# Attention masks and one table of query scales: loaded, or made on the chip from one row

## The chip, the cores and the metric

The kernel runs on one core of one Trainium2 chip. The metric is the device time of one execution in microseconds (us). Inputs lie in the chip's memory in the layouts that the host gave them; the host does no arithmetic on data.

## The reference, cut to what matters

```python
def _attn_ref(q, k, v):                     # (2, 8, 768, 64) each
    gamma = 1.0 - 2.0 ** (-5.0 - np.arange(H))
    for t in range(S):
        state = gamma * state + k[t] outer v[t]         # 64 x 64 per batch and head
        y[:, :, t] = scale * q[:, :, t] @ state
...
x = y as (1536 tokens, 512)
x = softplus(x @ moe_w_in) @ moe_w_out      # 512 -> 2048 -> 512
return silu(x @ moe2_w_in) @ moe2_w_out     # 512 -> 2048 -> 512
```

The first stage is retention: attention whose weight between token t and an earlier token s is gamma^(t-s), with one gamma for each of the eight heads. Two feed-forward layers follow.

## The kernel before

Retention is done in chunks of 128 tokens: two batches of six chunks are twelve tiles n = 0 to 11, n % 2 the batch, n // 2 the chunk. For each tile att_scores(n) (L263) multiplies keys by queries for the eight heads into two PSUM banks, four heads (one j of each head pair) in each; att_mask(n) (L271, VectorE) multiplies the two banks by mask[:, j], which holds scale * gamma^(t-s) for t >= s and 0 elsewhere; att_within(n) (L281) multiplies the result by the values; att_split(n) copies the sum out in two parts (L325 on ScalarE, L330 on VectorE). From chunk 1 on att_across (L303) adds what earlier chunks contribute: the queries, scaled by the table qs[c] (L215, on GpSimd for the early tiles), times the running state, which att_state (L243) sums from scaled keys (L230, factors in `cs`). att_turn_k (L223) turns the keys of the first tiles by a product with an identity, and ScalarE copies them out (L224). The scaled keys of tiles 0 and 1 come from GpSimd, later ones from VectorE.

The feed-forward layers follow (L529 and L569 the first; L679 and L713 the second), on weights that VectorE and ScalarE take apart from 64-bit floats (L427 to L474); the first weight tile is done between the masks and the key scales of tiles 2 and 3.

The order is written by hand (manual_schedule): each engine works through its instructions in the order of the code, and each waits for what it needs. All loads are issued from SP's queue, in the order of the code, at most eight ahead: the ninth waits until the first has landed, and so on. The first are

```python
att_load(0, 0, 2)                                # queries and keys of tile 0
nc.sync.dma_start(out=mask, in_=mask_d)          # 512 KB
att_load(1, 0, 2)
nc.sync.dma_start(out=cs, in_=cs_d)              # 24 KB
```

and behind them values and keys of tiles 0 and 1, queries and keys of 2 and 3, qs_load(1) (256 KB), and the first weight tile. While they are on their way TensorE runs WARM = 3 products of zeros (L889), 128 x 512 in float32, and GpSimd makes the identity (L877). Then, on TensorE: att_scores(0), att_turn_k(0), att_scores(1), att_within(0), att_within(1), att_scores(2), att_scores(3), att_state(0), att_state(1), att_within(2), att_within(3), att_across(2), att_state(2), att_state(3), and the first product of the first feed-forward layer.

att_scores(n) writes into the PSUM banks acc0 and acc1 for even n, acc2 and acc3 for odd n.

## Time and profile before

| | us |
|---|---|
| median of three runs | 562.45 (562.42 to 562.97) |
| the profiled execution | 562.56 |
| its span | 560.8 |
| TensorE busy in the span | 555.0 (99%) |
| VectorE busy | 346.8 (62%) |
| ScalarE busy | 295.1 (53%) |
| GpSimd busy | 39.1 (7%) |

Times in the rows below are microseconds from the start of the span. 1.8 us of the profiled execution lie outside its span. PE is TensorE and PEld its loading of weights, DVE is VectorE, ACT ScalarE, POOL GpSimd, SP the queue that issues the loads. A matrix product in float32 stands as two instructions. The ends of products are modelled, so that one that is followed at once by another is shown with an end that lies in the other; the distance between two starts is the safer number.

### The profile page before, as it was taken

How to read it: one execution, taken by the hardware profiler on the slowest of the kernel's cores; microseconds unless marked ns; L12 is line 12 of the kernel's file. 1: busy time of each engine (PE TensorE's matmuls, PEld its weight loads, DVE VectorE, ACT ScalarE, POOL GpSimd, SP SyncE). 2: the span in 40 equal slices, each digit the busy share in tenths (PEclk: the TensorE clock that was granted, in tenths of full speed). 3: DMA queues.
4: the chain of work that ended last, by engine and by line, in shares of the span. 5: the costliest groups of instructions: out<-in, count | busy, mean ns of one | idle time of the engine just before them, and what ended most of it. 6: DMA issues, size and time to landing. Idle time of an engine off the chain costs nothing.

```text
span 560.8 us, 8160 instructions
## 1 busy us (share of the span) xinstructions
PE 555.0 (99%) x3130; PEld 478.1 (85%) x3130; DVE 346.8 (62%) x618; ACT 295.1 (53%) x534; POOL 39.1 (7%) x56
## 2 busy tenths in 40 slices
PE   8999999999999999999999999999999999999997
PEld 6888888888888888888888989989889999999995
DVE  3999866699998989897953878525332221222113
ACT  2455535776776867876844867434524332332322
POOL 2321000010000101010200011000000000000000
PEclk9999999999999999999999999999999999999999
DMA  8993242497797678866835798764521554444412
GB/s 302 398 413 130 82 181 77 176 350 280 272 346 273 228 261 348 279 247 223 285 137 200 266 415 339 274 230 180 207 75 57 188 199 162 161 143 176 193 75 112
DMA packets 29062, 125.31 MB, mean 223 GB/s; under 512 B 3296, under 2 KB 3296, under 8 KB 25312
## 3 DMA queue, kind: packets, MB, share of 16 engines
q1 hardware_dynamic: 22752, 101.74, 49.0%
q0 software_dynamic: 6272, 23.07, 10.9%
q8 instruction: 24, 0.39, 0.3%
q14 instruction: 14, 0.11, 0.1%
HBM read 98.58 MB, written 26.21 MB: 223 GB/s over the span
## 4 chain that ended last, share of the span: by engine, by line
PE 97%; DMA 2%; SPq 0%; DVE 0%; issue 0%
PE acc L713 24%; PE h L529 24%; PE acc L569 23%; PE by L679 9%; PE bx L679 6%; PE bz L679 6%; DMA rp<-in_att 2%; PE py L281 2%; PE sc L263 1%; PE py L303 1%; PE state L243 1%; DVE rp L720 0%; SPq L858 0%; SPq L208 0%; SPq L393 0%
## 5 line engine op out<-in xcount | busy, mean ns | idle before, releaser
L529 PE MATMUL h<-rx,rw 128*128 128x512 f32 (+1 forms) x588 | 137.6, 386 | 0.0
L569 PE MATMUL acc<-rg,rw 128*128 128x512 f32 x564 | 134.6, 389 | 0.0
L529 PEld LDWEIGHTS h<-rx,rw 128*128 128x128 f32 x588 | 108.5, 188 | 22.4
L713 PE MATMUL acc<-rw,rg 128*128 128x512 f32 x477 | 125.3, 392 | 0.0
L569 PEld LDWEIGHTS acc<-rg,rw 128*128 128x128 f32 x564 | 105.7, 188 | 21.6 <-issue 0.2
L713 PEld LDWEIGHTS acc<-rw,rg 128*128 128x128 f32 x477 | 88.5, 188 | 12.6
L698 DVE TENSOR_TENSOR rg<-re,rg 128x384 fp32r<-128x384 f32 x53 | 29.4, 556 | 90.9 <-ACT re L696 90.9
L548 ACT ACTIVATE rg<-h 128x512 fp32r<-128x512 f32 x47 | 27.9, 595 | 65.0 <-PE h L529 51.1
L427 ACT ACTIVATE rc<-rc 128x512 f32<-128x512 f32 x58 | 38.5, 670 | 13.5 <-DMA rc<-in_wts 8.0
L445 DVE SCALAR_TENSOR_TENSOR rc<-rc 128x512 uint32<-128x512 uint32 x58 | 40.2, 693 | 2.0
L695 ACT ACTIVATE rg<-by 128x384 fp32r<-128x384 f32 x16 | 7.9, 491 | 54.2 <-PE by L679 54.2
L442 DVE TENSOR_SCALAR rc<-rc 128x512 uint32<-128x512 uint32 x64 | 27.4, 428 | 13.0 <-ACT rc L427 12.9
L768 DVE TENSOR_TENSOR rp<-bz,rp 128x384 f32<-128x384 f32 x16 | 8.9, 557 | 39.3 <-PE bz L679 39.3
L555 DVE TENSOR_TENSOR rg<-re,rg 128x512 fp32r<-128x512 f32 x47 | 32.1, 686 | 1.7 <-ACT re L549 1.6
L679 PE MATMUL by<-f,rw 128*128 128x384 f32 x144 | 29.2, 337 | 0.0
L679 PE MATMUL by<-rx,rw 128*128 128x384 f32 x144 | 29.2, 337 | 0.0
L448 DVE TENSOR_SCALAR rc<-rc 128x512 uint32<-128x512 uint32 x64 | 27.3, 427 | 2.2
L431 ACT ACTIVATE rc<-rc 128x1024 uint16<-128x1024 uint16 x27 | 28.5, 1055 | 0.0
L549 ACT ACTIVATE re<-h 128x512 f32<-128x512 f32 x48 | 28.4, 593 | 0.0
L679 PEld LDWEIGHTS by<-f,rw 128*128 128x128 f32 x144 | 25.9, 188 | 2.0
L679 PEld LDWEIGHTS by<-rx,rw 128*128 128x128 f32 x144 | 25.8, 188 | 2.2 <-ACT by L753 0.2
L474 ACT ACTIVATE rw<-rc 128x512 fp32r<-128x512 f32 x32 | 20.2, 632 | 13.2 <-DVE rc L445 13.2
(104 smaller groups left out, 699.1 us busy)
## 6 DMA issues: line engine op xcount, KB each, us to landing
rc<-in_wts SPq DMA_DIRECT2D x58, 512.0 KB, 4.5
rw<-d SPq DMA_DIRECT2D x13, 1792.0 KB, 7.3
rw<-d SPq DMA_DIRECT2D x14, 1024.0 KB, 9.1
near<-in_wts SPq DMA_DIRECT2D x21, 511.5 KB, 3.8
d<-st POOLq DMA_DIRECT2D x16, 512.0 KB, 6.0
d<-st POOLq DMA_DIRECT2D x8, 1024.0 KB, 5.1
rp<-in_att SPq DMA_DIRECT2D x8, 512.0 KB, 7.2
d<-w POOLq DMA_DIRECT2D x8, 512.0 KB, 3.8
```

The source lines that it names most:

```text
L427: nc.scalar.activation(out=z, in_=raw(u)[:, :, 1].bitcast(F32), func=AF.Copy, scale=2.0**-112)
L431: nc.scalar.activation(out=q[:, :, 0:2], in_=q[:, :, 1:3], func=AF.Copy)
L442: nc.vector.tensor_scalar(out=z, in0=z, scalar1=3, scalar2=4, op0=ALU.logical_shift_left, op1=ALU.bitwise_or)
L445: nc.vector.scalar_tensor_tensor(out=a, in0=hi, scalar=0x80000000, in1=z, op0=ALU.bitwise_and, op1=ALU.bitwise_or)
L529: nc.tensor.matmul(ph[:, t], lhsT=w[:, s], rhs=x[:, kc, t], start=kc == o == j == 0, stop=kc == NPAIR - 1 and j == 2, skip_group_check=i == 0,
L548: nc.scalar.activation(out=ghi, in_=ph, func=AF.Softplus)
L549: nc.scalar.activation(out=t, in_=ph, func=AF.Softplus)
L555: nc.vector.tensor_tensor(out=glo, in0=t, in1=ghi.bitcast(F32), op=ALU.subtract)
L569: nc.tensor.matmul(acc_t[m], lhsT=lhsT, rhs=rhs, start=first and j == 0 and not seeded, stop=last and j == 2, skip_group_check=m in SEEDED,)
L679: nc.tensor.matmul(to, lhsT=a[:, s], rhs=x[:, kc, :], start=start and kc == j == 0, stop=kc == 1 and j == 2, skip_group_check=True,)
L698: rest[c] = lambda: nc.vector.tensor_tensor(out=glo, in0=r, in1=ghi.bitcast(F32), op=ALU.subtract)
L713: nc.tensor.matmul(acc2_t[m], lhsT=a[:, s], rhs=b, start=start and j == 0, stop=stop and j == 2)
```

## The change

Neither the mask nor the query scales of chunk 1 are loaded. One partition's row of the mask (row 0: scale * gamma^t for every head, 4 KB) is loaded instead, from ScalarE's queue, and `cs` behind it from the same queue. A new function tables_make multiplies a row of ones by that row on TensorE, once for each j, which puts the row into all 128 partitions of a PSUM bank. VectorE makes from it and from `cs` the factor gamma^-s of each partition and head (`decay`) and multiplies; GpSimd puts zeros where t < s. ScalarE copies the row, one token further, as the query scales of chunk 1 into the two 64-partition halves, and VectorE makes their last column. The two banks are those of acc2 and acc3, which att_scores(1) takes next. WARM is 1, and att_turn_k(0) stands behind att_mask(1).

```diff
-WARM = 3
+WARM = 1
...
+    ones = rr[0:1, 1152 : 1152 + P]
+    decay = rr[:, 1280 : 1280 + H].rearrange("p (j a) -> p j a", j=2)
+    mask_row = rr[0:1, 8192:9216].rearrange("p (j t) -> p j t", j=2)
...
+    def rows_load():
+
+        nc.scalar.dma_start(out=mask_row, in_=mask_d[0:1].rearrange("p j a t -> p j (a t)"))
+        nc.scalar.dma_start(out=cs, in_=cs_d)
+
+    def tables_make():
+
+
+        grow = cs[:, H : 2 * H].rearrange("p (a j) -> p j a", j=2)
+        row = [psa.tile([P, NPAIR, P], F32, tag=f"acc{2 + j}", name=f"row{j}") for j in range(2)]
+        qs_t[1] = qs_ring.next()
+        qs = _rows(qs_t[1], NPAIR)
+        root = float(D) ** 0.5
+        for j in range(2):
+            nc.tensor.matmul(row[j], lhsT=ones, rhs=mask_row[:, j], start=True, stop=True)
+        for j in range(2):
+            r = slice(j * D, (j + 1) * D)
+            nc.vector.scalar_tensor_tensor(
+                out=decay[:, j], in0=row[j][:, :, 1], scalar=root, in1=grow[:, j], op0=ALU.mult, op1=ALU.mult
+            )
+            nc.vector.tensor_tensor(
+                out=mask[:, j],
+                in0=row[j],
+                in1=decay[:, j].rearrange("p (a o) -> p a o", o=1).to_broadcast([P, NPAIR, P]),
+                op=ALU.mult,
+            )
+            nc.scalar.activation(out=qs[r, :, : P - 1], in_=row[j][r, :, 1:], func=AF.Copy)
+            nc.vector.scalar_tensor_tensor(
+                out=qs[r, :, P - 1], in0=qs[r, :, P - 2], scalar=root, in1=row[j][r, :, 1], op0=ALU.mult, op1=ALU.mult
+            )
+            nc.gpsimd.affine_select(
+                out=mask[:, j],
...
     with tc.manual_schedule():
         att_load(0, 0, 2)
-        nc.sync.dma_start(out=mask, in_=mask_d)
         att_load(1, 0, 2)
-        nc.sync.dma_start(out=cs, in_=cs_d)
+        rows_load()
...
-        qs_load(1)
...
+        nc.vector.memset(ones, 1.0)
...
+        tables_make()
         att_scores(0)
         att_mask(0)
-        att_turn_k(0)
         att_scores(1)
         att_mask(1)
+        att_turn_k(0)
```

In the changed file lines stand further down: L263 is L306 there, L223 L266, L271 L314, L281 L324, L230 L273.

On TensorE the program begins before the change as follows (sc0 and sc1 are the scores of tiles 0 and 1, their second number is j; kn0 the turned keys of tile 0, py0 and py1 the outputs of att_within).

```order
L889 MATMUL warm_119<-rr_76 128x512 x3
L263 MATMUL sc0_0_123<-rp_67 128x128
...
L263 MATMUL sc0_1_124<-rp_67 128x128
L223 MATMUL kn0_135<-rr_76,rp_67 128x128 x4
L263 MATMUL sc1_0_141<-rp_67 128x128
...
L263 MATMUL sc1_1_142<-rp_67 128x128
L281 MATMUL py0_153<-rr_76,rp_67 64x128 x8
L281 MATMUL py1_166<-rr_76,rp_67 64x128 x8
```

And after it:

```order
L931 MATMUL warm_119<-rr_76 128x512
L221 MATMUL row0_121<-rr_76 128x512
L221 MATMUL row1_122<-rr_76 128x512
L306 MATMUL sc0_0_135<-rp_67 128x128
...
L306 MATMUL sc0_1_136<-rp_67 128x128
L306 MATMUL sc1_0_147<-rp_67 128x128
...
L306 MATMUL sc1_1_148<-rp_67 128x128
L266 MATMUL kn0_159<-rr_76,rp_67 128x128 x4
L324 MATMUL py0_165<-rr_76,rp_67 64x128 x8
L324 MATMUL py1_178<-rr_76,rp_67 64x128 x8
```

Two warm-up products have given way to the two row products, and the turned keys stand behind the scores of tile 1.

On VectorE, between the clearing of rr_76 and the first copy of an output, with what each waits for (DMAHW: a transfer; row0 and row1 are the two banks), stands after the change:

```order
L224 SCALAR_TENSOR_TENSOR rr_76<-row0_121,cs_72 128x4 [waits DMAHW2_49,PE_49]
L227 TENSOR_TENSOR rr_76<-row0_121,rr_76 128x512 [waits DVE_49]
L234 SCALAR_TENSOR_TENSOR rr_76<-rr_76,row0_121 64x4 [waits Activation_49]
L224 SCALAR_TENSOR_TENSOR rr_76<-row1_122,cs_72 128x4 [waits PE_49]
L227 TENSOR_TENSOR rr_76<-row1_122,rr_76 128x512 [waits DVE_49]
L234 SCALAR_TENSOR_TENSOR rr_76<-rr_76,row1_122 64x4 [waits Activation_49]
L314 TENSOR_TENSOR rr_76<-sc0_0_135,rr_76 128x512 [waits PE_49,Pool_49]
L314 TENSOR_TENSOR rr_76<-sc0_1_136,rr_76 128x512 [waits PE_49,Pool_49]
```

Before, the two mask products of tile 0 were the first work behind the clearing; now six instructions stand ahead of them, and they wait for GpSimd too, where before the first of them waited for the mask's transfer.

ScalarE begins after the change with (the table load was first before):

```order
L209 DMA rr_76<-in_mask 1x1024
L210 DMA cs_72<-in_cs 128x48
L915 ACT_TABLE_LOAD
L233 ACTIVATE rr_76<-row0_121 64x4x127 [waits DVE_49]
L233 ACTIVATE rr_76<-row1_122 64x4x127 [waits DVE_49]
L267 ACTIVATE rp_67<-kn0_159 128x512 [waits PE_49]
```

Two issues stand ahead of the table load, and two copies of the rows, each behind VectorE's mask product of the same bank, ahead of the copy of the turned keys.

## Rows read from the trace of the kernel before

**Rows 1.** Busy time by stretch; columns: stretch, length, engines, granted clock, DMA share, GB/s.
```profile
1.46:6.52 5.06, 5.06 (x7) 1.85 (x7) 0.00 (x0) 0.57 (x1) 0.00 (x0) 1.00 0.88 277
6.52:15.73 9.21, 8.73 (x138) 7.73 (x137) 6.01 (x10) 2.58 (x5) 4.08 (x4) 1.00 1.03 380
15.73:21.00 5.27, 5.23 (x97) 4.74 (x97) 5.09 (x10) 3.54 (x6) 0.50 (x1) 1.00 1.03 401
21.00:540.00 519.00, 519.00 (x2813) 449.34 (x2814) 329.85 (x590) 282.81 (x514) 33.79 (x46) 1.00 0.61 225
```

**Rows 2.** The chain of waits of 0 to 22 us: start, length, what.
```profile
1.65 6.20 DMA rp<-in_att
...
8.24 7.36 DMA rp<-in_att
```

**Rows 3.** TensorE's timeline: start, length, instructions [idle time before them, releaser].
```profile
1.46 5.13 PE L889 MATMUL warm<-rr 128*128 128x512 f32 x6 [1.46 <-DVE rr L875]
6.52 1.16 PE L263 MATMUL sc<-rp 64*128 64x128 f32 x16
7.61 1.16 PE L223 MATMUL kn<-rr,rp 128*128 128x128 f32 x8
8.70 1.16 PE L263 MATMUL sc<-rp 64*128 64x128 f32 x16
9.79 2.53 PE L281 MATMUL py<-rr,rp 128*64 128x128 f32 x32
12.25 1.16 PE L263 MATMUL sc<-rp 64*128 64x128 f32 x16
...
15.73 1.09 PE L281 MATMUL py<-rr,rp 128*64 128x128 f32 x16 [0.34 <-DMA rp<-in_att]
...
17.62 1.96 PE L303 MATMUL py<-rr 64*64 64x128 f32 x32
19.52 0.93 PE L243 MATMUL state<-rp,rr 128*64 128x64 f32 x15
```

**Rows 4.** Waits of 0 to 21 us: who for whom, sum in us, times, longest.
```profile
PEld sc L263 <- issue: 1.3, 2, 1.1
...
PE py L281 <- DMA rp<-in_att: 0.3, 1, 0.3
...
PEld state L243 <- DVE rr L230: 0.2, 1, 0.2
```

**Rows 5.** VectorE's timeline of the same stretch.
```profile
12.99 0.69 DVE L330 TENSOR_TENSOR rx<-py,rx 128x512 fp32r<-128x512 f32 x1 [0.73 <-ACT rx L325]
13.60 2.48 DVE L271 TENSOR_TENSOR rr<-sc,rr 128x512 f32<-128x512 f32 x4
...
18.68 0.69 DVE L230 TENSOR_TENSOR rr<-rp,cs 128x512 f32<-128x512 f32 x1
```

**Rows 6.** SP's timeline: start of an issue, its length.
```profile
0.74 0.38 SPq L208 DMA_DIRECT2D rp<-in_att  x1
...
2.12 0.52 SPq L860 DMA_DIRECT2D cs<-in_cs  x1
```

**Rows 7.** DMA issues of the first 1 and 2.5 us: count, KB each, us to landing.
```profile
rp<-in_att SPq DMA_DIRECT2D x1, 512.0 KB, 4.5
...
cs<-in_cs SPq DMA_DIRECT2D x1, 24.0 KB, 5.9
```

**Rows 8.** What the DMA engines moved, 0 to 10 us in 40 slices of 0.25 us.
```profile
GB/s 0 0 0 0 0 0 0 180 115 295 246 213 246 180 262 328 311 279 295 344 328 410 377 377 410 349 402 373 288 231 241 156 221 336 410 401 426 418 410 467
```

**Rows 9.** Groups of instructions of 0 to 16 us: count, busy us, mean ns, idle before.
```profile
L271 DVE TENSOR_TENSOR rr<-sc,rr 128x512 f32<-128x512 f32 x8 | 5.1, 684 | 7.2 <-PE sc L263 7.2
...
L224 ACT ACTIVATE rp<-kn 128x512 f32<-128x512 f32 x1 | 0.6, 597 | 6.8 <-PE kn L223 6.8
...
L877 POOL TENSOR_SCALAR_AFFINE_SELECT rr<-rr 128x128 f32<-128x128 f32 x1 | 0.3, 292 | 0.1
```

More of the change, by code (lines that the diff above doesn't have):

```diff
@@ L202, in qs_load @@
         nc.sync.dma_start(out=qs_t[c], in_=qs_d[c])
+    def rows_load():
[26 more added lines that the diff above has]
+                out=mask[:, j],
+                in_=mask[:, j],
+                compare_op=ALU.is_ge,
+                fill=0.0,
+                base=0,
+                pattern=[[0, NPAIR], [1, P]],
+                channel_multiplier=-1,
+            )
     def att_load(n, lo=0, hi=4):
```

## The prediction, made before the changed kernel ran

> **What bounds the kernel now.** I read four views in this order. First the busy time by stretch [rows 1]: from 21 us to 540 us TensorE is busy 519.00 of 519.00 us, so nothing that happens on another engine or queue there can be seen in the time, and whatever moves the first 21 us moves the end by the same amount. Between 6.52 and 21 us TensorE is idle 0.52 us in all (9.21 less 8.73, 5.27 less 5.23). Before 6.52 us it runs only the three warm-up products on zeros. Second the chain of waits of the first 22 us [rows 2]: it is laid through two loads from `in_att`, 6.20 and 7.36 us long, up to 15.6 us. That reads as if the loads bound the start. Third the TensorE timeline and the waits [rows 3, 4], which show that this is only half of it: the load held TensorE 0.3 us at 15.73 us, and next to it TensorE was as good as full. Fourth VectorE [rows 5]: it stands 0.73 us until ScalarE has copied the output of token tile 1, starts the subtraction at 12.99 us, and from 13.60 us works on without a pause to L230 at 18.68 us, for which TensorE waits at 19.52 us (0.2 us, [rows 4]). So two chains end at 19.5 us: the loads, which let go at 15.73 us, and "att_within(1) ends, ScalarE, VectorE", which starts where TensorE goes over to att_scores(2), at 12.25 us [rows 3]. To gain, a change must bring both forward; to lose, it is enough to delay one.
>
> **The bytes taken off the SP queue.** The mask (512 KB) and the query scales of chunk 1 (256 KB) are gone, 0.79 MB. At the 380 GB/s of 6.52 to 15.73 us [rows 1] that is 2.1 us, so the loads behind them land about 1.3 us (behind the mask) to 2.1 us earlier. What this is worth: the 0.3 us stall at 15.73 us, if TensorE comes there as early as now. What is late next is VectorE, at 19.52 us, so of the 2.1 us nearly nothing is left. SP's other loads move up with it and wait for less. GpSimd's first query scaling no longer waits for a load; its result is wanted only by att_across(2) at 17.6 us, so this is worth 0.
>
> **The warm-up.** Three products of 128 x 512 in float32 stand as six instructions in 5.13 us, 0.855 us each, 1.71 us a product [rows 3]. L223 right behind them runs eight instructions of 128 columns between 7.61 and 8.70 us, 0.545 us for 512 columns. So the warm-up runs at the lower of TensorE's two levels (1.2 GHz) and the work behind it above that, although the granted clock reads 1.00 in both stretches [rows 1]. WARM = 1 takes out two products, 3.42 us. tables_make puts in two products of the same 512 columns (one row deep instead of 128). Taken at the warm-up's price, as the nearest row with the same columns at that place, they cost 3.42 us again: the sum is zero, if the first can start when the single warm-up ends, at 1.46 + 1.71 = 3.17 us.
>
> **When it can start.** It waits for the mask's first row, 4 KB on ScalarE's queue, which is issued as SP's first load is, at about 0.74 us [rows 6]. Bytes first move in the slice that starts at 1.75 us [rows 8], 1.0 us after the first issue. From the last byte to the landing: by the sums of [rows 8] (slices of 0.25 us) 524 KB had moved at about 4.0 us, and the first load (524 KB, issued at 0.74 us, 4.5 us on its way [rows 6, 7]) landed at 5.24 us, so 1.2 us. The least is therefore 0.74 + 1.0 + 1.2 = 2.94 us, hidden by the warm-up; the most, if it goes at the pace of the full load beside it, is 5.24 us, 2.1 us after the warm-up. I take 0.4 us of sharing, 3.35 us, nearer to the low end because only 4 KB have to move. The second transfer, `cs`, took 5.9 us behind 1.57 MB in SP's queue [rows 7]; now it is issued at about 1.15 us and lands between 3.35 us (1.0 + 1.2 later) and 7.05 us (5.9 later). It is wanted when the first row product is done, 3.35 + 1.71 + 0.07 = 5.13 us. I take it as just in time; each microsecond later costs one.
>
> **The chain that makes the tables.** Per half: a VectorE product of 4 columns, a mask product of 512 columns (0.68, the mean of L271 [rows 9]), a ScalarE copy (0.60, as L224 [rows 9]), a VectorE fix of 4 columns. The waits order them strictly: the ScalarE copy waits for the mask product, the fix for the copy. No row has a VectorE instruction of 4 columns: between 0 and the 0.68 of 512 columns, I take 0.16, near the low end for its size. With 0.18 for the hand-overs (0.03 to 0.05 each, from the gap between 7.68 us, when att_scores(0) ends, and the next engine's starts) a half is 1.78 us. The first half, from 5.13 us, ends at 6.91 us, as the second row product does (3.35 + 3.42 + 0.07 = 6.84 us): almost hidden. The second half is open: 6.84 + 1.78 = 8.62 us. Who waits for it: att_scores(1) writes into the two banks of the row products, so its second matmul stands until the second fix. TensorE has done att_scores(0) by 7.9 us and idles 0.7 us there. Behind it, in TensorE's queue, stands everything else.
>
> **The masks' triangles.** Two GpSimd selections of 512 columns. The only row is 128 columns in 0.292 us [rows 9]; times four 1.17 us. The second starts at about 7.8 us and is done at 9.0 us; VectorE asks for it at 9.3 us (fixes done at 8.62 us, then the first product of att_mask(0), 0.68), and att_within(1) does not need the last mask product before 11.7 us where VectorE can give it at 11.3 us. Cover 0.3 + 0.4 us: the selection would have to take about 2 us to cost anything.
>
> **The sum.** 8.62 us; the other 15 of 16 matmuls of att_scores(1) 1.02 (of 1.09, [rows 3]) gives 9.64; att_turn_k(0), which now stands behind it, 1.09 gives 10.73; att_within(0) and (1) 1.89 (what att_within(2) and (3) take without a wait between them, 15.73 to 17.62 us [rows 3]) and the 0.2 us pause of issue before att_scores(2) (1.3 less 1.1, [rows 4]) give 12.82 us, against 12.25 us. That is 0.57 us later. VectorE's row from 12.99 to 19.5 us starts at that point and has no gap to give it back, and behind 21 us TensorE has none either. Profiled execution: 562.56 + 0.57 = **563.1 us**. The median of the three runs is 562.45, 0.11 below it; I leave that in the range.
>
> **A page of the skill beside it.** The transfers on ScalarE's queue decide the sum, and no row shows a small one beside a full SP queue. The Trainium skill, DMA: Bandwidth & Descriptors (Queues, rings and completion order), says that each DMA engine takes turns between the queues it has work for, a packet at a time. By that rule both small transfers would pass SP's bytes and land near the low ends, the row product would start at 3.17 us, and the sum would be 562.9 us (0.18 less).
>
> **The rivals.**
> - *The small transfers come late.* Place: TensorE in front of the row products, or VectorE's first product for `cs`. For it: loads issued in the first 3 us took 4.5 to 5.9 us [rows 7], and the DMA engines move no more than 277 GB/s in that stretch [rows 1]. Against it: they are small. Price: one to one from 3.17 us for the row and from about 5.1 us for `cs`. It decides, slower by more than 0.2% (1.12 us, about what a measurement of this kernel can tell from no change), from a landing at about 3.9 us or 5.7 us. A row at 4.5 us gives 564.3; the ends (5.24, 7.05) give 565.0 and 565.0.
> - *TensorE's clock stays low longer.* Now the engine works without a break from 1.46 to 6.5 us before it runs faster. After the change it pauses up to 0.2 us at 3.2 us and 0.7 us at 7.9 us, and the row products fill one row of the array. If the faster level comes only behind that, att_scores(1), att_turn_k(0) and att_within(0) and (1) (1.02 + 1.09 + 1.89 = 4.0 us) run up to 1.57 times as long (0.855 against 0.545, [rows 3]): up to +2.3 us, 565.4; att_scores(1) alone, +0.6, 563.7. The Trainium skill, TensorE: Matmul & The Clock Gate (What's actually happening), says that the slow level is the default and activity releases it; by that the two pauses count against the change.
> - *The loads were the bound after all.* The chain of waits speaks for it [rows 2], and then up to 2.1 us come off: 560.5. Against it: in front of 15.73 us TensorE has only 0.5 us of idle time to close [rows 1], and the new chain adds a pause. At best the row products start at 3.17 us, run faster at their end and the stall goes: 562.0, which is within 0.2%.
> - *GpSimd's selection takes over 2 us*, from which it decides; at 2.5 us each the second ends at 11.4 us where 9.7 us (9.0 and the cover) would do: 1.7 us late, 564.8.
>
> **How the numbers follow.** The forecast with its neighbours within 0.2%: 0.60. Late transfers 0.21, of which 0.17 slower by more; low clock 0.11, of which 0.09; slow selection 0.05, all of it; loads as the bound 0.03, faster by more. That is 0.60 + 0.04 + 0.02 = 0.66 within 0.2%, 0.17 + 0.09 + 0.05 = 0.31 slower, 0.03 faster. The range goes from 562.0 (nothing waits and the stall goes) to 564.8, which holds most of the late transfers and leaves out the last 0.1 of late and low clock at their full prices.
>
> **What would show it.** In the changed profile: L221's first matmul at 3.2 to 3.5 us, released by a transfer; L306 broken after its first half by a wait of about 0.7 us for VectorE (L234); att_scores(2) at 12.8 us; no wait for `in_att` at att_within(2); L273 on VectorE at about 19.2 us; TensorE full from 21.5 us. If L221 stands at 4 us or later, or its decay product waits for `in_cs`, the first rival is right; if L266 takes much over 1.09 us, the second.

## The result, and the profile after

| | before | after |
|---|---|---|
| median, us | 562.61 (562.42 to 562.97) | 565.65 (564.95 to 566.43) |
| runs | 6 | 6 |
| profiled execution, its span | 562.56, 560.8 | 566.43, 564.7 |

The ratio is 1.0055, 95% interval 1.0042 to 1.0067: slower by 3.04 us. The forecast was 563.1 us with a range to 564.8; both are too low. The profiled execution of after is the slowest of its six, 0.8 us over the median, so its trace shows somewhat more loss than the median has.

The lines of the code have moved: the row products are L221, att_scores L306, att_turn_k L266, att_within L324, att_state L286, the first feed-forward product L572; on VectorE the decay product is L224, the mask product L227, the fix of the last column L234, att_mask L314, the key scales L273, the weight tile L481 to L506; on GpSimd the selection is L237, the query scaling L258.

TensorE's timeline of after, against [rows 3] (start, length, instructions, idle time before them and who ended it):

```profile
1.52 2.07 PE L931 MATMUL warm<-rr 128*128 128x512 f32 x2 [1.52 <-DVE rr L916]
3.53 3.78 PE L221 MATMUL row<-rr 1*128 1x512 f32 x4
7.24 4.71 PE L306 MATMUL sc<-rp 64*128 64x128 f32 x32
11.88 1.92 PE L266 MATMUL kn<-rr,rp 128*128 128x128 f32 x8
13.73 1.97 PE L324 MATMUL py<-rr,rp 128*64 128x128 f32 x32
15.63 1.16 PE L306 MATMUL sc<-rp 64*128 64x128 f32 x16
...
22.70 0.69 PE L286 MATMUL state<-rp,rr 128*64 128x64 f32 x16 [0.20 <-DVE rr L273]
...
48.09 2.08 PE L572 MATMUL h<-rx,rw 128*128 128x512 f32 x8 [0.58 <-DVE rx L373]
```

The distances between starts tell it. The line at 7.24 us holds att_scores(0) and (1); of att_scores(1), 14 of the 16 instructions stand behind the wait for the tables, as the chain of waits has them:

```profile
9.88 2.07 PE sc L306 x14
```

They take 2.00 us up to 11.88 us. att_turn_k(0), eight instructions, takes 1.85 us (13.73 less 11.88) where it took 1.09 [rows 3]. The products of att_within(0) and (1) behind it take 1.90 us, as those of att_within(2) and (3) do in [rows 3] (1.89). So TensorE ran at the lower of its two levels (1.2 GHz) until some point near 13.5 us, and not until 6.5 us as before. att_scores(2) starts at 15.63 us instead of 12.25, att_state(2) at 22.70 instead of 19.52: 3.4 and 3.2 us. At 48.09 us a stall of 0.58 us is added; behind 21 us the kernel before has none [rows 1]. Together 3.8 of the 3.9 us by which the two spans differ.

The granted clock does not show any of this. Two stretches of after, with the same columns as [rows 1]:

```profile
7.24:11.88 4.64, 4.50 (x34) 3.98 (x33) 2.83 (x8) 1.18 (x2) 1.27 (x2) 1.00 1.03 415
...
24.00:540.00 516.00, 515.29 (x2794) 445.69 (x2795) 331.77 (x590) 281.32 (x510) 33.77 (x46) 1.00 0.60 223
```

The granted clock reads 1.00 in the first of them, in which the products run at the lower level; the level has to be read from the time between starts. In the second, TensorE is idle 0.71 us, where [rows 1] have none.

VectorE's timeline of after, the tables:

```profile
6.51 0.16 DVE L224 SCALAR_TENSOR_TENSOR rr<-row,cs 128x4 f32<-128x4 f32 x1 [4.92 <-DMA cs<-in_cs]
...
8.05 0.15 DVE L234 SCALAR_TENSOR_TENSOR rr<-rr,row 64x4 f32<-64x4 f32 x1 [0.65 <-ACT rr L233]
8.13 0.15 DVE L224 SCALAR_TENSOR_TENSOR rr<-row,cs 128x4 f32<-128x4 f32 x1
...
9.65 0.17 DVE L234 SCALAR_TENSOR_TENSOR rr<-rr,row 64x4 f32<-64x4 f32 x1 [0.66 <-ACT rr L233]
```

VectorE waits for `cs` until 6.4 us. It was issued at 1.35 us and took 5.05 us, as the chain of waits of after has it:

```profile
1.35 5.05 DMA cs<-in_cs
```

The second fix is done at 9.82 us. TensorE (its weight load, PEld) waits for it only 0.4 us, since it is itself late:

```profile
PEld sc L306 <- DVE rr L234: 0.4, 1, 0.4
```

Last, VectorE and GpSimd behind 24 us in after. VectorE first, then GpSimd:

```profile
25.09 1.68 DVE L482 SCALAR_TENSOR_TENSOR rc<-rc 128x512 uint32<-128x512 uint32 x1
...
27.13 0.69 DVE L488 SCALAR_TENSOR_TENSOR rc<-rc 128x512 uint32<-128x512 uint32 x1
...
46.55 1.48 DVE L373 TENSOR_TENSOR rx<-rr,rx 128x512 fp32r<-128x512 f32 x1 [1.11 <-ACT rx L368]
```

```profile
24.73 1.49 POOL L258 TENSOR_TENSOR rr<-rp,rr 128x512 f32<-128x512 f32 x1
...
46.18 1.30 POOL L258 TENSOR_TENSOR rr<-rp,rr 128x512 f32<-128x512 f32 x1 [6.78 <-PE sc L306]
```

L482, an instruction of the form of L488 (0.69 us), takes 1.68 us while GpSimd scales queries, and an instruction of att_split (L373) takes 1.48 instead of 0.69 us just ahead of the stall at 48.09 us. So there are three suspects: the level of TensorE's clock, the late `cs`, and the meeting of VectorE and GpSimd further on.

### The profile page after: what moved, and what is told of

It reads as the page before. It is cut to its first block, busy times and chain, and to the rows that moved or that the text cites. A ratio compares the mean times of both kernels' runs of the same rounds, so it can differ in the third digit from the quotient of the medians.

```text
span 564.7 us, 8175 instructions
## 1 busy us (share of the span) xinstructions
PE 558.3 (99%) x3130; PEld 480.2 (85%) x3130; DVE 350.5 (62%) x625; ACT 296.3 (52%) x536; POOL 40.8 (7%) x58
## 4 chain that ended last, share of the span: by engine, by line
PE 96%; DVE 2%; DMA 1%; ACT 1%; issue 0%; ACTq 0%; DVEq 0%
PE acc L756 23%; PE h L572 23%; PE acc L612 23%; PE by L722 9%; PE bx L722 6%; PE bz L722 6%; PE py L324 2%; PE sc L306 1%; DMA cs<-in_cs 1%; PE py L346 1%; PE state L286 1%; DVE rr L314 0%; PE kn L266 0%; DVE rx L373 0%; DVE rr L227 0%
## 5 line engine op out<-in xcount | busy, mean ns | idle before, releaser
L572 PE MATMUL h<-rx,rw 128*128 128x512 f32 (+1 forms) x588 | 137.8, 386 | 0.7 <-DVE rx L373 0.6
L572 PEld LDWEIGHTS h<-rx,rw 128*128 128x128 f32 x588 | 108.5, 188 | 23.4 <-DVE rx L373 0.9
L741 DVE TENSOR_TENSOR rg<-re,rg 128x384 fp32r<-128x384 f32 x53 | 29.3, 555 | 90.8 <-ACT re L739 90.8
L591 ACT ACTIVATE rg<-h 128x512 fp32r<-128x512 f32 x47 | 27.9, 594 | 64.3 <-PE h L572 51.3
L488 DVE SCALAR_TENSOR_TENSOR rc<-rc 128x512 uint32<-128x512 uint32 x58 | 40.2, 692 | 2.0
```

The lines of the kernel that those rows point to most:

```text
L488: nc.vector.scalar_tensor_tensor(out=a, in0=hi, scalar=0x80000000, in1=z, op0=ALU.bitwise_and, op1=ALU.bitwise_or)
L572: nc.tensor.matmul(ph[:, t], lhsT=w[:, s], rhs=x[:, kc, t], start=kc == o == j == 0, stop=kc == NPAIR - 1 and j == 2, skip_group_check=i == 0,
L591: nc.scalar.activation(out=ghi, in_=ph, func=AF.Softplus)
L741: rest[c] = lambda: nc.vector.tensor_tensor(out=glo, in0=r, in1=ghi.bitcast(F32), op=ALU.subtract)
```

## Experiments on TensorE's level

The theory is that the row products, one row deep, do not bring the faster level nearer as the warm-up products with 128 rows do. The rivals are the pauses that the change puts in, the late `cs`, and the new order.

**k1_warm: the kernel before, its three warm-up products one row deep.** No tables, no change of loads.

```diff
-            nc.tensor.matmul(warm, lhsT=zero[:, :P], rhs=zero, start=True, stop=True)
+            nc.tensor.matmul(warm, lhsT=zero[:1, :P], rhs=zero[:1], start=True, stop=True)
```

> The kernel before, with one edit: its three warm-up products are one row deep instead of 128 (the same 512 columns, the same number, no pause). Nothing else changes, so the time tells what the depth of a product does to TensorE's clock. Theory A (the faster level is fed by how full the array works, and one-row products feed it little or not at all): att_scores(0), att_turn_k(0) and att_scores(1) run at the lower level, about 1.9 us each where they took 1.09, so about +2 us, 564.6. Theory B (in the changed kernel it was the pauses at 3.2 and 8.9 us that kept the level low): no pause here, no change, 562.6 and 1.09 us each.

Measured: 565.52 us (565.38 to 565.62) against 562.62, ratio 1.0052 (1.0035 to 1.0069). TensorE's timeline:

```profile
1.46 5.48 PE L889 MATMUL warm<-rr 1*128 1x512 f32 x6 [1.46 <-DVE rr L875]
6.87 2.08 PE L263 MATMUL sc<-rp 64*128 64x128 f32 x16
8.87 2.07 PE L223 MATMUL kn<-rr,rp 128*128 128x128 f32 x8
10.88 1.67 PE L263 MATMUL sc<-rp 64*128 64x128 f32 x16
...
29.12 3.00 PE L529 MATMUL h<-rx,rw 128*128 128x512 f32 x12 [0.80 <-DVE rw L463]
```

Fewer rows in products whose result nobody uses cost 2.9 us, 0.9 us more than theory A had set. The first att_scores and att_turn_k take 2.00 and 2.01 us between starts instead of 1.09 each; the faster level comes in att_scores(1), and no pause stands ahead of it. att_scores(2) starts at 14.94 us instead of 12.25. Then there is a stall of 0.80 us at 29 us, to which the last group of experiments comes back; it is part of the 2.9 us.

**warm1: the kernel before with WARM = 1.** Only full-depth products, but fewer, and a pause.

```diff
-WARM = 3
+WARM = 1
```

> The kernel before, with WARM = 1 alone: one full-depth warm-up product from 1.5 to 3.2 us, then a pause until the first load lands at about 5.2 us, then the same work as before. Theory B (a pause keeps the clock low): att_scores(0), att_turn_k(0) and att_scores(1) at 1.9 us each, which eats the 1.3 us of the earlier start and more: 563.5 to 564.5. Theory A (only the depth matters; real products count): the level rises about when it did, the earlier start of 1.3 us is kept in part: 561.5 to 562.6.

Measured: 562.85 us (562.57 to 563.49), ratio 1.0007 (0.9997 to 1.0016).

```profile
5.27 2.08 PE L263 MATMUL sc<-rp 64*128 64x128 f32 x16 [1.74 <-DMA rp<-in_att]
7.28 2.04 PE L223 MATMUL kn<-rr,rp 128*128 128x128 f32 x8
9.25 1.16 PE L263 MATMUL sc<-rp 64*128 64x128 f32 x16
```

One full-depth product and a pause of 1.74 us do not bring the level up either: two steps take 2.01 and 1.97 us. But here the work starts 1.25 us earlier than in [rows 3], since no warm-up stands in front of it, and the time does not change. **warm2**, the same with WARM = 2:

```diff
-WARM = 3
+WARM = 2
```

> The kernel before with two warm-up products instead of three; loads and tables untouched. They end at 4.9 us, the first load lands at 5.24 us. If the level still rises near 6.5 us: att_scores(0) starts at 5.3 us, partly at the lower level, and the work before att_within(2) moves up by 0.5 to 0.9 us, of which the loads (in_att until 15.7 us) leave 0 to 0.3: 562.3 to 562.6. If the pause of 0.3 us or the missing product keeps it low: att_turn_k(0) at 2.0 us, 562.9 to 563.5.

Measured: 562.56 us (562.32 to 563.05), ratio 0.9999 (0.9989 to 1.0008). att_turn_k(0) takes 1.21 us between starts there, so the level is up by about 8 us, but the work then waits for loads, 0.42 us of it at 12.55 us in front of att_scores(2). So one or two of the three warm-up products of the kernel before can go without a change of its time that can be measured.

**deep32: the row products 32 deep.** `cs` first on SP's queue (this is cs_sp, below); the mask row is loaded into 32 partitions, and the row of ones is 32 rows of 1/32.

```diff
-    ones = rr[0:1, 1152 : 1152 + P]
-    mask_row = rr[0:1, 8192:9216].rearrange("p (j t) -> p j t", j=2)
+    ones = rr[0:DEEP, 1152 : 1152 + P]
+    mask_row = rr[0:DEEP, 8192:9216].rearrange("p (j t) -> p j t", j=2)
...
-        nc.vector.memset(ones, 1.0)
+        nc.vector.memset(ones, 1.0 / DEEP)
```

> cs as SP's first transfer, as in the run cs_sp, and the mask's first row loaded into 32 partitions instead of one (128 KB instead of 4), so that the two row products are 32 rows deep (factors of 1/32; the sums are the same numbers). Theory A (depth feeds the faster level): with a quarter of the array full either the level rises near 6.5 us as before the change, att_scores(0) and (1) take 1.09 us each, att_scores(2) starts at about 12.8 us instead of 13.81 and the time is about 563.3; or a quarter does not suffice, and it is cs_sp again (565.2, att_scores(0) near 1.9 us). If depth has nothing to do with it: cs_sp again, plus what the larger load delays.

Measured: 565.33 us (564.54 to 565.89), ratio 1.0051 (1.0034 to 1.0067); cs_sp, one row deep, has 1.0050. att_scores(2) starts at 13.69 us against 13.81. A quarter of the rows changes nothing that can be measured.

**k64_warm: the kernel before, warm-up 64 deep.**

```diff
-            nc.tensor.matmul(warm, lhsT=zero[:, :P], rhs=zero, start=True, stop=True)
+            nc.tensor.matmul(warm, lhsT=zero[:64, :P], rhs=zero[:64], start=True, stop=True)
```

> The kernel before with its three warm-up products 64 rows deep instead of 128. One row deep cost 2.9 us; 32 rows deep (in the changed kernel) gained nothing over one. If what feeds the faster level grows with depth and half suffices: att_scores(0) at 1.09 us, 562.6. If half does not suffice: att_scores(0) and att_turn_k(0) at 2.0 us each as with one row, 565.5; in between (part of the products behind them at the lower level) 563.5 to 565.

Measured: 562.91, 565.71, 565.62, 565.37 and 565.82 us. These are two values and no mean: the first is that of the kernel before, the others that of k1_warm. The trace is of the first run; in it the last 14 of the 16 instructions of att_scores(0) take 1.82 us up to the start of att_turn_k(0), which takes 1.08 us itself:

```profile
6.74 1.89 PE L263 MATMUL sc<-rp 64*128 64x128 f32 x14
8.56 1.16 PE L223 MATMUL kn<-rr,rp 128*128 128x128 f32 x8
```

At half depth the faster level came in this run by about 8.6 us, later than the 6.5 us of the kernel before, and the times of the four others, 2.5 to 2.9 us longer, are those of a kernel in which it did not. They have no trace, so that is not shown, and why the runs part is open.

**deep128: the row products 128 deep, in the changed kernel.** deep32 with the other 96 rows of the moving operand filled by zeros, which changes no sum. The edit against deep32:

```diff
-    ones = rr[0:DEEP, 1152 : 1152 + P]
+    ones = rr[:, 1152 : 1152 + P]
...
+        nc.vector.memset(row_flat[64:], 0.0)
+        nc.gpsimd.memset(row_flat[DEEP:64], 0.0)
```

> deep32 with the rows of the array below the 32 filled by zeros (two memsets, one on VectorE and one on GpSimd, which both stand idle there), so that the row products are 128 deep like the warm-up, at the same place, with the same columns and the same sums. Theory A (the depth of the products decides when the faster level comes): with full depth from 1.5 us on, the level changes about 5 us later as in the kernel before, inside or just behind the row products: these take 3.2 to 3.75 us, the first half of att_scores 1.1 instead of 2.0 us, TensorE then idles 0.5 to 0.8 us for the second fix (about 8.9 us), and att_scores(2) starts at 13.0 to 13.2 us instead of 13.69. Rival (it is the place or the new pauses, not the depth): the first half of att_scores keeps 2.0 us and att_scores(2) stays at 13.7. Time: by A about 564.7 us with the VectorE stall behind 25 us, 563.5 without; by the rival 565.3 as deep32.

Measured: 564.28 us (562.82 to 565.01, 10 runs), ratio 1.0024 (1.0013 to 1.0034). Four runs lie at 562.8 to 563.0, six at 564.2 to 565.0. TensorE's timeline, of a run of the first kind:

```profile
3.74 3.47 PE L222 MATMUL row<-rr 128*128 128x512 f32 x4
7.14 1.62 PE L307 MATMUL sc<-rp 64*128 64x128 f32 x18
9.19 1.16 PE L307 MATMUL sc<-rp 64*128 64x128 f32 x14 [0.43 <-DVE rr L235]
10.27 1.16 PE L267 MATMUL kn<-rr,rp 128*128 128x128 f32 x8
...
13.26 1.16 PE L307 MATMUL sc<-rp 64*128 64x128 f32 x16
```

At the same place, with the same columns, the same chain and a pause in front of it, the level rises in this run between 7.1 and 8.8 us: the first 18 instructions of att_scores take 1.6 us (16 take 2.0 in turn_back, at the lower level), the next 14 1.08 us between starts, where after has 2.00 (9.88 to 11.88). Against deep32, from which it differs in the depth (and the two memsets) alone, the interval begins lower and ends where the other begins (1.0034), and four of its ten runs lie below 563.1 us, where the lowest of deep32 is 564.54. So the depth of the products, more than the place or the pauses, is what held the level down in deep32. The six upper runs have no trace; the last group comes back to what divides the ten.

How late the level comes without full depth varies from trace to trace: by the steps between starts about 10 us in cs_sp and deep32, about 12 us in k1_warm and turn_back, near 13.5 us in after and later still in no_q45. It is latest in the two in which att_scores(1) waits for the tables (0.4 and 0.74 us). Whether these pauses add to the delay no run shows by itself.

## Experiments on `cs`, the chain and the order

**cs_sp: after, with `cs` issued first on SP's queue.**

```diff
     def rows_load():
...
-        nc.scalar.dma_start(out=cs, in_=cs_d)
...
+        nc.sync.dma_start(out=cs, in_=cs_d)
         att_load(0, 0, 2)
```

> The changed kernel with cs as the first transfer of SP's queue instead of the second of ScalarE's. If the late landing of cs (6.40 us, where the first row product is done at about 5.4 us) is on the path: the first decay product starts at 5.4 to 5.6 us, the second fix ends 0.7 us earlier (9.1 instead of 9.82 us), and so does everything behind: 564.9. If the low clock alone sets the place (att_scores(0) is done at 8.9 us only): between 0 and 0.7, and no gain at all if the row products are late by as much: 565.6.

Measured: 565.2 us (564.8 to 566.26), ratio 1.0050 (1.0035 to 1.0065). `cs` lands 1.8 us after its issue, VectorE starts when the first row product is done, at 5.63 us, and the second fix is over at 9.05 us. TensorE:

```profile
7.23 3.66 PE L305 MATMUL sc<-rp 64*128 64x128 f32 x32
10.83 1.16 PE L265 MATMUL kn<-rr,rp 128*128 128x128 f32 x8
...
13.81 1.16 PE L305 MATMUL sc<-rp 64*128 64x128 f32 x16
...
28.27 2.99 PE L571 MATMUL h<-rx,rw 128*128 128x512 f32 x12 [1.06 <-DVE rw L505]
```

att_scores(2) starts 1.8 us earlier than in after, as the tables come 0.8 us earlier and the faster level is there for att_turn_k(0) (1.08 us). A stall of 1.06 us at 28 us is new, and the median gains 0.45 us, less than the measurement tells apart.

**turn_back: after, with att_turn_k(0) between the two att_scores,** where the kernel before has it.

```diff
         att_mask(0)
+        att_turn_k(0)
         att_scores(1)
         att_mask(1)
-        att_turn_k(0)
```

> The changed kernel with att_turn_k(0) back between att_scores(0) and att_scores(1), one part of the change undone. The wait for the second fix (0.9 us at 8.9 us) is then filled by the turned keys. Theory A: they run at the lower level (1.85 us) up to 10.8 us, att_scores(1) behind them: 0.9 us earlier in all, 564.8. Theory B: with the pause gone the level rises some 1 to 2 us earlier too, att_scores(1) takes 1.09 instead of 2.0 us: 563.8. A rival for both, the waits behind it are on VectorE anyway: no change, 565.6.

Measured: 565.63 us (565.21 to 565.96), ratio 1.0054 (1.0039 to 1.0069). That is the time of the rival, though not for its reason: att_scores(2) starts at 15.21 instead of 15.63 us, and a stall of 0.71 us at 29.31 us is new. At the lower level there is hardly a pause that att_turn_k could fill.

**qs_later: deep32 with the row products in two other banks and the fixes behind att_mask(0),** so that att_scores(1) waits for no table.

```diff
-        row = [psa.tile([P, NPAIR, P], F32, tag=f"acc{2 + j}", name=f"row{j}") for j in range(2)]
+        row = [ps.tile([P, NPAIR, P], F32, tag="py", name=f"row{j}") for j in range(2)]
...
-        tables_make()
+        last = tables_make()
         att_scores(0)
         att_mask(0)
+        last()
```

> deep32, and the chain of the tables shortened: the row products go into two other banks, so that att_scores(1) does not wait for the second fix, and the two fixes stand behind att_mask(0). What is left on the path is row product, decay, mask product, selection. If the level rises near 6.5 us: att_scores(0) and (1) without a break from 7.0 to 9.2 us, att_scores(2) at about 12.4 us, no wait for in_att at att_within(2): 562.5 to 562.9, level with the kernel before. If it does not: att_scores(2) at 13.8 us, 564.5 to 565. In neither case faster than before by what can be measured, since TensorE's own work from 7.0 us on is what it was from 6.5 us on.

Measured: 565.7 us (564.77 to 565.92), ratio 1.0051 (1.0036 to 1.0066). TensorE's timeline is that of deep32 again: att_scores(0) at 7.23, att_scores(2) at 13.69 us. The expected 564.5 to 565 was low. With the level low TensorE is slower than the tables, and their chain bounds nothing here.

**warm3_cs: cs_sp with WARM = 3 again.** The rows and tables come later, but behind a full warm-up.

```diff
-WARM = 1
+WARM = 3
```

> cs_sp (tables made on the chip, cs first on SP's queue) with three full-depth warm-up products ahead of the row products, as before the change had them. Theory A: the faster level comes at about 6.5 us; the row products then take about 1.0 us each instead of 1.86, att_scores(0) 1.09 instead of about 1.9, and they are done at about 9.5 us; the second fix falls at about 11 us and holds att_scores(1); att_scores(2) starts near 15.3 us, later than the 13.81 of cs_sp, so slower: 566.5. If depth of the warm-up were nothing: rows and scores as slow as in cs_sp behind a later start, att_scores(2) near 17 us, 568.

Measured: 565.24, 567.84, 565.5 and 568.52 us, ratio 1.0072 (1.0045 to 1.0100). The trace is of the first run:

```profile
5.83 1.98 PE L220 MATMUL row<-rr 1*128 1x512 f32 x4
7.74 1.49 PE L305 MATMUL sc<-rp 64*128 64x128 f32 x18
10.35 1.16 PE L305 MATMUL sc<-rp 64*128 64x128 f32 x14 [1.13 <-DVE rr L233]
...
28.76 2.98 PE L571 MATMUL h<-rx,rw 128*128 128x512 f32 x12 [0.93 <-DVE rw L505]
```

Behind a full-depth warm-up the same four row instructions take 1.91 us between starts instead of 3.71: the level was up, and their price was that of the level. Now the chain of tables is what TensorE waits for (1.13 us). The traced run lies 1.3 us below the expected 566.5, as att_scores(2) starts at 14.42 us where 15.3 was set; the median of the four, 566.67, meets it only through two upper runs. These two, above 567 us, with a mean granted clock of 0.994 instead of 1.00, remain unexplained.

## Experiments on the stalls further on

In k1_warm, cs_sp, turn_back, deep32, qs_later and warm3_cs a stall of 0.7 to 1.1 us stands in front of the feed-forward product at 27.9 to 29.3 us, and VectorE, the releaser, has two instructions of the weight tile stretched to 1.3 to 1.8 us ahead of it, beside GpSimd's scaling of the queries of tiles 4 and 5. In cs_sp, VectorE and then GpSimd:

```profile
22.99 1.78 DVE L481 SCALAR_TENSOR_TENSOR rc<-rc 128x512 uint32<-128x512 uint32 x1
24.69 1.51 DVE L484 TENSOR_SCALAR rc<-rc 128x512 uint32<-128x512 uint32 x1
```

```profile
22.93 1.29 POOL L257 TENSOR_TENSOR rr<-rr 128x512 f32<-128x512 f32 x1 [5.69 <-DMA rr<-in_qs]
24.18 1.74 POOL L257 TENSOR_TENSOR rr<-rp,rr 128x512 f32<-128x512 f32 x1
```

In the kernel before, the same two GpSimd instructions lie beside att_mask, which is not stretched (2.49 us for four):

```profile
25.16 2.49 DVE L271 TENSOR_TENSOR rr<-sc,rr 128x512 f32<-128x512 f32 x4 [0.51 <-PE sc L263]
```

```profile
24.90 1.28 POOL L215 TENSOR_TENSOR rr<-rr 128x512 f32<-128x512 f32 x1 [8.68 <-DMA rr<-in_qs]
26.14 1.31 POOL L215 TENSOR_TENSOR rr<-rp,rr 128x512 f32<-128x512 f32 x1
```

The kernel before has stretched instructions too, at other places and without a stall of TensorE: L330 at 35.38 us takes 1.25 us, L438 at 47.88 us 1.52 us, both beside GpSimd's scalings. So it matters which instruction is met. The next kernels leave the two GpSimd instructions of tiles 4 and 5 out.

**no_q45: after without them.** In the function that scales the queries of tile n:

```diff
+        if n in (4, 5):
+            qp_t[n] = _rows(a_t[n][:, 0, :], NPAIR)
+            return
```

> The changed kernel without GpSimd's two query scalings of tiles 4 and 5, whose queries go unscaled into att_across(4) (left out; two GpSimd instructions of 1.3 us, nothing on another engine). In the changed kernel they run at 23.5 to 26.2 us, beside VectorE's work on a weight tile, of which one instruction took 1.68 us instead of 0.69; before they ran at 24.9 to 27.5 us beside the masks, and none was stretched. Theory C (this collision makes VectorE late by 1.0 us, for which TensorE pays at 48 us): no stretched instruction at 25 us, the 0.6 us stall at 48 us gone or much smaller, time 0.6 to 0.9 less, 564.9. Rival: other GpSimd instructions stretch VectorE elsewhere and the stall stays: 565.6.

Measured: 566.47 us (565.41 to 566.77), ratio 1.0064 (1.0049 to 1.0079). The stall at 48 us is gone, but in the profiled run `cs` came at 7.0 us instead of 6.4, and att_scores(2) at 16.64 us instead of 15.63. The time decides nothing: two things changed, one by chance.

**cs_no_q45: cs_sp without them.** Here `cs` does not come behind a full queue; the edit is the same, made in cs_sp.

> cs_sp without GpSimd's query scalings of tiles 4 and 5 (left out; those queries go unscaled). The same edit on the changed kernel took away the stretched VectorE instructions between 25 and 27 us and TensorE's stall at 48 us, but its transfers of cs came later, so its time told nothing; here cs is early. Theory C: the stall of 1.06 us at 28 us, which TensorE has behind a weight tile on VectorE, is gone; time 0.8 to 1.1 less than cs_sp, 564.2. Rival: VectorE is late there without GpSimd too, and 565.2 stays.

Measured: 563.93 us (563.49 to 565.88, 10 runs), ratio 1.0027 (1.0018 to 1.0036), against 1.0050 (1.0035 to 1.0065) with them. TensorE's start is that of cs_sp, and the stall is gone:

```profile
13.77 1.16 PE L308 MATMUL sc<-rp 64*128 64x128 f32 x16
...
27.10 3.02 PE L574 MATMUL h<-rx,rw 128*128 128x512 f32 x12
```

So of the 2.6 us that cs_sp loses, the meeting of the two engines makes about 1.3 us, half; the two intervals just touch, so the share is rough. With the two gone GpSimd reaches the scalings of tiles 6 and 7 earlier, so these move as well.

**deep128_turn: deep128 with att_turn_k(0) between the two att_scores,** by the edit of turn_back.

> deep128 with att_turn_k(0) put back between the two halves, where the kernel before has it. Theory A: with the faster level at about 7 us, the order matters again: turn_k (1.09 us) fills the idle time for the second fix, att_scores(1) starts at about 9.4 us and att_scores(2) at 12.3 to 12.6 us, as in the kernel before (12.25); the time is 562.9 to 564.2, according to whether the VectorE stall behind 25 us comes (0.6 to 1.2 us). Rival (place or pauses): as turn_back, att_scores(2) at 13.5 us or later, about 565.3 us.

Measured: 564.35 us (562.74 to 564.61, 10 runs), ratio 1.0028 (1.0018 to 1.0037); two runs at 562.7 to 562.8, eight at 564.0 to 564.6. The trace is of the first kind. TensorE's start has no pause left, and one VectorE instruction of the weight tile is stretched, where cs_sp has two, without a stall of TensorE:

```profile
7.25 1.16 PE L307 MATMUL sc<-rp 64*128 64x128 f32 x16
8.35 1.16 PE L267 MATMUL kn<-rr,rp 128*128 128x128 f32 x8
...
12.99 1.16 PE L307 MATMUL sc<-rp 64*128 64x128 f32 x16
```

```profile
24.41 1.64 DVE L507 SCALAR_TENSOR_TENSOR rw<-rc 128x512 fp32r<-128x512 int32 x1
```

At the faster level the order gives 0.27 us (12.99 against 13.26), which the time does not show.

**deep_turn_no45: deep128_turn without the two GpSimd instructions,** by the edit of no_q45.

> deep128_turn without the two GpSimd query scalings of tiles 4 and 5 (their products read the unscaled queries: two GpSimd instructions of 1.3 to 1.5 us are left out, nothing else). deep128_turn gave two values, 562.7 to 562.8 twice and 564.0 to 564.6 eight times; its trace, of a run of the lower kind, has a VectorE instruction stretched to 1.64 us beside the first of these two at 24.4 us and no stall of TensorE. Theory C (in the runs of the upper kind VectorE is held up by these two at a point where TensorE waits for it): without them all runs lie at the lower value, 562.4 to 562.9. Rival (the upper value comes from TensorE's level at the start, as with the warm-up half as deep): both values stay, most runs at 564.0 to 564.6.

Measured: 563.35 us (562.89 to 563.87, 10 runs) against 562.68, ratio 1.0007 (0.9998 to 1.0017): no difference from the kernel before that can be measured. The group at 564.0 to 564.6 is gone, with the level up as early (att_turn_k(0) takes 1.09 us, and att_scores(2) starts at 13.29 us against 12.99), so the upper value goes with these two GpSimd instructions. That the level has no part in it is not shown: cs_no_q45, with the level low and the two left out, has runs from 563.49 us up, among those of this kernel, and no run with the upper value has a trace. Beside cs_no_q45 (1.0018 to 1.0036) the interval is lower by a hair: with these scalings out, the low level and the other order still cost something like 0.6 us by the medians. The expected 562.4 to 562.9 was a little low. The scalings of tiles 6 and 7 have moved up and meet VectorE instead:

```profile
35.83 2.98 PE L576 MATMUL h<-rx,rw 128*128 128x512 f32 x12 [0.34 <-DVE rw L510]
```

## Why the prediction was wrong, point by point

- **The step that failed** is "Taken at the warm-up's price, as the nearest row with the same columns at that place, they cost 3.42 us again: the sum is zero". As a price it was nearly right: 3.71 us for the two (7.24 less 3.53). But the warm-up's products do a second thing that has no price in their own row: TensorE runs faster behind them. The one-row products that took their place do not do this, and the sum had no term for it. k1_warm, which makes this exchange alone in the kernel before, for all three products, loses 2.9 us, 0.80 us of it by a stall further on that the delay brings with it; after loses 3.04. deep128, which differs from deep32 in the depth, has runs of 562.8 us again, where deep32 has none below 564.5. The loss is not that two warm-up products are missing: warm1 leaves two out and stays at 562.85 us, since its real work starts at 5.27 us and runs at the faster level from about 9 us. In after the row products keep TensorE until 7.24 us, and the faster level comes near 13.5 us.
- **The rival was named and sized, and not believed.** "TensorE's clock stays low longer" gave the reason (one row of the array, pauses) and up to 2.3 us for att_scores(1), att_turn_k(0) and att_within. By the trace of after: att_scores(1) 2.00 us where 1.02 was set (for 15 of its 16 instructions; 14 stand behind the wait), att_turn_k(0) 1.85 where 1.09, att_within(0) and (1) with the pause 1.90 where 2.09; together 1.55 us. It got a chance of 0.11, and the range left out its full price. [rows 3] held the hint: nothing but those full-depth products stands in front of the change from 0.855 to 0.545 us for 512 columns. The Trainium skill, TensorE: Matmul & The Clock Gate (What's actually happening), was cited for the pauses; warm1, whose level is low behind one product and a pause of 1.74 us, agrees. If every product counts as activity, k1_warm does not agree: TensorE works there without a pause from 1.46 us, and the level is low until about 12 us. That products of few rows leave it low is shown by k1_warm and deep32 alone.
- **`cs` just in time** was mis-sized. It landed at 6.40 us, within the bounds (3.35 to 7.05), where it was wanted at about 5.6; the second fix came at 9.82 instead of 8.62 us. By itself it cost TensorE a wait of 0.4 us. Bringing it forward (cs_sp) moved att_scores(2) by 1.8 us and the median by 0.45. The rule of the Trainium skill, DMA: Bandwidth & Descriptors (Queues, rings and completion order), from which the prediction took that both small transfers would pass SP's bytes, fits the 4 KB row (its product began at 3.53 us, without a wait in the profile). What was taken from it for `cs`, 5.05 us on its way, did not come.
- **The start, 15.63 us instead of the forecast 12.82, adds up**: rows done 0.40 us late (7.24 for 6.84) and hidden, the second fix 1.20 late, the hand-over to TensorE 0.06, the three steps above 1.55: 2.81 us. From there to the end the stall of 0.58 us comes on top, and 0.2 us is given back by 22.70 us (3.18 us late instead of 3.38).
- **"Behind 21 us TensorE has none either"** was wrong in what it left out. That TensorE is full there means that nothing can be gained, not that nothing can be lost: VectorE, shifted by some us against GpSimd, met it at other instructions. [rows 1] gives VectorE 329.85 of 519 us there, which hides that it is 24.34 of 27 us busy from 21 to 48 us. cs_no_q45 puts this at about 1.3 us in cs_sp. In after's trace it is the 0.58 us at 48.09 us; how much of the median of after it is, no run shows (no_q45 was not decisive). The forecast had put GpSimd's first scaling at 0 and had no term for the others.
- **Right:** the loads were not the bound (no wait for `in_att` at att_within(2) in after, nor in deep128_turn, where TensorE is there only 0.2 us later than before, and no gain from 0.79 MB less); a VectorE instruction of 4 columns takes 0.16 us; half of the chain takes 1.69 us (6.51 to 8.20, 8.13 to 9.82) where 1.78 was set; att_scores(1) is what waits for the second fix; the row product began at 3.53 us where 3.35 was set. The selection took 0.63 us where 1.17 was set, which its cover made harmless.

The two losses do not add up simply. cs_sp, turn_back, qs_later and deep32 start att_scores(2) 0.4 to 1.9 us earlier than after, yet their medians all stay within 565.2 to 565.7 us: each has a new stall of 0.7 to 1.1 us at 28 to 29 us. With the scalings out and the level low (cs_no_q45) 1.3 us of loss are left; with the row products at full depth and the scalings in (deep128, deep128_turn) fourteen of twenty runs lose 1.5 to 2.5 us and six about 0.5 at most. Only with both put right (deep_turn_no45, interval 0.9998 to 1.0017) can the loss no longer be told from none.

## What to carry to other kernels

Before a warm-up is replaced by useful work of the same length, ask whether that work does the same to TensorE's level: compare the rows of the array that its products fill, and read the level from the time between starts behind it, not from the granted clock. If few rows are needed, zeros in the other rows cost little (here two memsets on idle engines), and in the traced runs the faster level came early with them. And when a chain is shifted against another engine, look behind the shift for instructions of VectorE and GpSimd that both work from SBUF: a full TensorE can still lose there.

## What the runs showed of the hardware that was not expected

- Products of the same columns and nearly the same length (1.7 to 1.9 us each) left TensorE at the lower level when 1 or 32 rows deep (k1_warm, after, deep32), and let it rise when 128 deep, zeros included (the kernel before, the traces of deep128 and deep128_turn); at 64 rows the runs of one kernel fell on both times (562.9 and 565.4 to 565.8 us).
- VectorE instructions of 0.42 and 0.69 us take 1.3 to 1.8 us while GpSimd multiplies two operands. att_mask, one of whose operands is in PSUM, kept its 0.62 us each beside the same instructions (25.16 us in the kernel before). The Trainium skill, SBUF — State Buffer (Who interferes with whom), says that a VectorE instruction with two SBUF inputs contends with a GpSimd instruction that reads SBUF, and that one of the two then blocks. The traces agree, with 1.68 us for 0.69 (L482 above). Instructions with one SBUF input, of which that sentence does not speak, were stretched too: L484 in cs_sp takes 1.51 us where its form takes 0.42.
- `cs`, 24 KB for 128 partitions, took 5.05 to 5.67 us from ScalarE's queue beside a full SP queue, and 1.8 us as the first transfer of SP's queue (cs_sp; 2.4 to 2.8 us in deep32, deep128, deep128_turn and deep_turn_no45, where ScalarE's queue carries 128 KB beside it).
